# Linear attention and a gated feed-forward net on one core: output by seven half-block products, tails loaded together, a new order

## The chip, the cores and the metric

The kernel runs on one core of one Trainium2 chip. A core has a matrix engine (TensorE, "PE" in the profile, with its weight loads as "PEld"), VectorE ("DVE"), ScalarE ("ACT"), GpSimd ("POOL") and SyncE ("SP"), which here only issues transfers; 16 DMA engines serve the transfer queues. Each engine executes its own instructions in order and waits on semaphores for the others. The metric is the time of one execution in microseconds (us). A lower time is better.

## What is computed

```python
# q, k, v: [8 batches, 8 heads, 576 positions, 64]
phi = lambda x: np.where(x > 0, x, np.exp(x) - 1.0) + 1.0
q_p, k_p = phi(q), phi(k)
kv  = einsum('bhsd,bhse->bhde', k_p, v)      # one 64x64 matrix per batch and head
z   = k_p.sum(axis=2)
x   = einsum('bhsd,bhde->bhse', q_p, kv) / (einsum('bhsd,bhd->bhs', q_p, z)[..., None] + 1e-6)
x   = x.transpose(0, 2, 1, 3).reshape(4608, 512)
a, b = x @ w1, x @ w2                        # 512 -> 1024 each
out  = ((a * b) @ w3) @ w_out                # 1024 -> 1024 -> 512
```

Inputs and the output are float32, 28.3 MB of q, k and v, 10.5 MB of weights and 9.4 MB of output; the products run in bfloat16.

## The kernel before

**Tiling.** A batch has 576 positions: 512 main ones and a tail of 64. The main positions of batch b are chunk b (0 to 7), 512 rows of x; the eight tails make chunk 8. The partition of a main row is position // 4, so that a load has runs of 1 KB.

**Steps.** The program is one long written list of steps, `ORDER`; `manual_schedule` takes each engine's instructions in exactly that order, and the function `step` maps a token to a function. A token is a letter, a batch or chunk number, and an index; one `+` behind it moves a step from its first engine to the next (ScalarE to VectorE for copies, SyncE to GpSimd for loads).

- `M`, `L`, `N` (load_qkv, L92): q, k, v of four heads' main rows, 512 KB each, into the pool `ld` of 13 buffers. `R` (load_tail, L99): tails of one batch. `C`, `E`, `B`: w_out, w3 and column blocks of w1 and w2, all on GpSimd's queue, which converts to bfloat16 on the way.
- `x`/`X`, `y`/`Y`, `z`/`Z` (L164 to L199): phi of k (small letter) or q (capital) as min(exp(x), max(x, 0) + 1): an exponential on ScalarE, a two-operation scalar instruction on VectorE, and a minimum on VectorE. Index 2 is the tail of q and k in one tile.
- `v`: v to bfloat16, with a column of ones beside each head, which gives z in the same matmuls. `K` (kv_full, L216): kv and z of a batch, two heads per matmul. `T`, or `a` through TensorE: phi(q) transposed (T is a DMA transpose on SyncE's queue). `A` (nat, L262): the attention of 128 positions, four matmuls, then 1e-6 added, a reciprocal and a multiplication on VectorE. `D`, or `P` through TensorE: x transposed.
- `w`, `u` (L132, L139): w3 transposed and multiplied with w_out, so that (h @ w3) @ w_out needs only one folded matrix `wf_sb` of 1024x512.
- `F` (f_unit): 128 of the 1024 columns of a and b for a chunk: eight matmuls of 128x512 into two of four PSUM banks, a copy of a on ScalarE (L327) and a multiplication on VectorE (L328). `h` and `i` do the same for F0.0 and F0.1 in quarters.
- `O` (o_unit, L475): 128 rows of the output: eight matmuls of 128x512 over the 1024 columns, and a copy out of PSUM (L481). `S`, `H`: store of two or one row blocks; `Q` (L497): one row block in two halves of 256 columns.

**What sets the order.** SyncE issues its loads, the transposes and the stores strictly in the written order, each behind the wait of the one ahead. GpSimd issues a load once the transfer eight places earlier on its queue has landed. A buffer of a pool is taken round robin and only when its last reader is done. `GATES` names pairs of loads of which the first must wait for the landing of the second; it is empty here.

The file holds functions that the list of this kernel doesn't call: `V` (w_unit, L448), `s` (s_make, L416) and `t` (wt_make, L151) among them. They compute the output of a chunk by Strassen's method in Winograd's form: the 1024 columns of h and the 512 of the output are halved, and so are the 512 rows, and seven products of half blocks replace eight.

Of the kernel before, what the change touches and what calls it, by code (L numbers as in the profile page):

```python
# [8 lines left out]
F32 = mybir.dt.float32  # L9
# [11 lines left out]
def kernel(  # L21
# [24 lines left out]

    consts = ctx.enter_context(tc.tile_pool(name="consts", bufs=1))
    wpool = ctx.enter_context(tc.tile_pool(name="weights", bufs=1))
    ld = ctx.enter_context(tc.tile_pool(name="ld", bufs=13))
    ldr = ctx.enter_context(tc.tile_pool(name="ldr", bufs=3))  # L50
# [4 lines left out]
    xt_p = ctx.enter_context(tc.tile_pool(name="xt", bufs=3))  # L55
# [15 lines left out]
    vrs = [wpool.tile([P, 2, 2, 2, E1], BF16, name=f"vr{i}") for i in range(2)]  # L71
# [5 lines left out]
    def constants(part, alt):  # L77
        if part == 0:
            make_identity(nc, ident)
        else:  # L80
            eng = nc.vector if alt else nc.gpsimd
            for t in (vrs[part - 1], kvs[part - 1]):
                eng.memset(t, 0.0)
            eng.memset(vts[part - 1][..., D:E1], 1.0)
            for g in range(2):
                eng.memset(vrs[part - 1][g * R:(g + 1) * R, :, g, :, D:E1], 1.0)
# [12 lines left out]
    def load_tail(b, part, alt):  # L99
        names = ("qk", "v")[part]  # L100
        t = raw[names + "r", b] = ldr.tile([P, len(names), RW], F32, tag="ldr" + names, name=names + "32r")
        for i, name in enumerate(names):
            for g in range(2):
                ins = (nc.gpsimd if alt else nc.sync).dma_start(  # L104
                    out=t[g * R:(g + 1) * R, i].rearrange("p (h d) -> p h d", d=D),
                    in_=src[name][b, g * 4:(g + 1) * 4, NJ * P:S, :].rearrange("h p d -> p h d"))
# [50 lines left out]
    ph, es = {}, {}  # L157

    def part_of(name, b, g):
        if g == 2:  # L160
            return raw["qkr", b].rearrange("p i x -> p (i x)"), 2 * RW, "r"
        return raw[name, b, g], HW, ""

    def phi_exp(name, b, g):  # L164
        x, w, r = part_of(name, b, g)
        e = e_p.tile([P, w], BF16, tag="e" + r, name="e" + r, bufs=2 if r else 4)
        es[name, b, g] = e
        nc.scalar.activation(out=e, in_=x, func=AF.Exp)  # L168

    def phi_max1(name, b, g, alt):  # L170
        x, w, r = part_of(name, b, g)
        y = es["y", name, b, g] = e_p.tile([P, w], BF16, tag="y" + r, name="y" + r, bufs=2)
        (nc.gpsimd if alt else nc.vector).tensor_scalar(  # L173
            out=y, in0=x, scalar1=0.0, scalar2=1.0, op0=ALU.max, op1=ALU.add)

    def phi_tile(name, b):
        p = ph.setdefault((name, b), [None, None])
        if p[0] is None:
            w = JW + (2 * RW if name == "q" else 0)
            t = phi_p.tile([P, w], BF16, tag=name + "j", name=name + "j", bufs=1 if name == "k" else 2)  # L180
            p[0] = t[:, 0:JW].rearrange("p (c j u d) -> p c j u d", j=NJ, u=2, d=D)
            if name == "q":
                p[1] = t[:, JW:JW + RW]
                ph["qt", b] = t
                ph.setdefault(("k", b), [None, None])[1] = t[:, JW + RW:JW + 2 * RW]
        return p

    def phi_min(name, b, g):
        x, w, r = part_of(name, b, g)
        e, y = es[name, b, g], es["y", name, b, g]  # L190
        if g == 2:
            phi_tile("q", b)
            nc.vector.tensor_tensor(out=ph["qt", b][:, JW:JW + 2 * RW], in0=e, in1=y, op=ALU.min)
            return
        p = phi_tile(name, b)
        e, y = (t.rearrange("p (c u j d) -> p c u j d", c=2, u=2, d=D) for t in (e, y))
        for c in range(2):
            nc.vector.tensor_tensor(out=p[0][:, 2 * g + c].rearrange("p j u d -> p u j d"),  # L198
                                    in0=e[:, c], in1=y[:, c], op=ALU.min)  # L199

    def v_unit(b, i, alt):
        vt, vr = vts[b % 2], vrs[b % 2]
# [4 lines left out]
        else:  # L207
            for g in range(2):
                rows = slice(g * R, (g + 1) * R)
                copy_of(alt)(out=vr[rows, :, g, :, 0:D], in_=raw["vr", b][rows, 0].rearrange(  # L210
                    "p (i u d) -> p i u d", i=2, d=D))
# [4 lines left out]
    def kv_full(b, alt):  # L216
        kj, kr = ph["k", b]
        vt, vr, kv = vts[b % 2], vrs[b % 2], kvs[b % 2]
        kvp = at_ps.tile([P, 2, NCH], F32, tag="at", name="kvp")
        W = 2 * E1  # L220
        for i in range(2):
            for g in range(2):
                hp = 2 * g + i
                for j in range(NJ):
                    nc.tensor.matmul(kvp[:, i, g * W:(g + 1) * W],  # L225
                                     kj[:, hp, j].rearrange("p u d -> p (u d)"),
                                     vt[:, j, 2 * hp:2 * hp + 2, :].rearrange("p h e -> p (h e)"),
                                     start=(g == 0 and j == 0), stop=False, skip_group_check=True)
# [435 lines left out]
```

## Time and profile before

| | |
|---|---|
| time, median of 3 runs (lowest, highest) | 259.99 us (259.03, 260.37) |
| time of the profiled execution | 259.34 us |
| its span, first to last instruction | 257.4 us |
| granted TensorE clock, mean | 0.993 |
| busy: TensorE, VectorE, ScalarE, GpSimd | 232.3, 159.1, 116.8, 49.1 us |
| first matmul, first F, first K | 13.15, 40.70, 26.01 us |
| last matmul ends | about 252.6 us |

The page splits the span into 40 slices of 6.4 us and gives a digit, the busy share in tenths, for each engine. Groups put the instructions of one line and shape together, with total busy time, mean duration of one, and the idle time ahead of them with what ended it. Matmuls overlap in the records: a 128x512 one lasts 380 ns there, but the next starts 216 ns later. A window's row gives, behind its length, the busy time of PE, PEld, DVE, ACT and POOL with the number of instructions, the granted clock, the DMA share and GB/s.

### The profile page before, as it was taken

The page shows a single profiled execution, that of the slowest core. Times are in us where ns is not written, and L with a number is a line of the kernel's source. Part 1 is how long each engine was busy: PE and PEld are TensorE (multiplying, and loading weights), DVE is VectorE, ACT ScalarE, POOL GpSimd, SP SyncE. Part 2 cuts the span into 40 slices and gives each one's busy share as a digit, 9 for nine tenths or more (in the row PEclk, how much of TensorE's full clock was granted, in tenths as well). Part 3 has the DMA queues.
Part 4 walks back from the last instruction along what each step waited for, and adds up shares of the span by engine and source line. Part 5 has one row for each costly group of instructions (what it writes and reads, how often), then busy time and mean ns, then how long its engine had stood idle before and what let it go on. Part 6 is the DMA issues. An engine that isn't in the chain of part 4 may idle for free.

```text
span 257.4 us, 3788 instructions
## 1 busy us (share of the span) xinstructions
PE 232.3 (90%) x1352; PEld 117.8 (46%) x1368; DVE 159.1 (62%) x350; ACT 116.8 (45%) x180; POOL 49.1 (19%) x84
## 2 busy tenths in 40 slices
PE   0087899999999869999999999999999999999992
PEld 0063565554454434445445445454544444444540
DVE  0548589778899426897887899978235633343200
ACT  1404677357756506755562473645332312332221
POOL 8524479455045100600000000000000000000000
PEclk9999999999999979999999999999999999999999
DMA  6999999999989999799999998646512143001124
GB/s 220 211 237 289 311 255 245 200 248 283 299 247 291 194 242 347 182 284 222 356 308 211 289 263 272 154 89 151 200 20 91 74 83 163 3 0 30 42 115 139
DMA packets 63762, 50.57 MB, mean 196 GB/s; under 512 B 33536, under 2 KB 58368, under 8 KB 63744
## 3 DMA queue, kind: packets, MB, share of 16 engines
q1 hardware_dynamic: 54432, 37.10, 55.9%
q0 software_dynamic: 9152, 13.11, 23.4%
q8 instruction: 10, 0.16, 0.3%
q10 hardware_dynamic: 160, 0.13, 0.2%
q14 instruction: 8, 0.07, 0.1%
HBM read 38.80 MB, written 9.44 MB: 187 GB/s over the span
## 4 chain that ended last, share of the span: by engine, by line
PE 78%; DMA 13%; DVE 4%; issue 2%; ACT 0%; POOL 0%; DVEq 0%; ACTq 0%; POOLq 0%
PE a_ps L322 24%; PE b_ps L322 23%; PE o_ps L479 21%; DMA v<-in_v_dram 5%; DMA qt<-qj 4%; PE nd L280 4%; DMA wt_sb<-in_moe_w_out_dram 4%; PE kvp L225 2%; PE wf_ps L143 1%; PE kvp L229 1%; DVE y L173 1%; DVE vt L204 1%; PE o_ps L504 1%; DVE kj L198 1%; DVE qj L198 0%
## 5 line engine op out<-in xcount | busy, mean ns | idle before, releaser
L322 PEld LDWEIGHTS <-w_sb 128*128 128x128 bf16 x576 | 55.3, 98 | 61.8 <-issue 0.9
L328 DVE TENSOR_TENSOR ab<-a_sb,b_ps 128x512 bf16<-128x512 f32 x72 | 49.1, 685 | 38.2 <-PE b_ps L322 30.5
L322 PE MATMUL a_ps<-xt,w_sb 128*128 128x512 bf16 x256 | 67.3, 382 | 0.0
L322 PE MATMUL b_ps<-xt,w_sb 128*128 128x512 bf16 x256 | 66.7, 379 | 0.0
L327 ACT COPY a_sb<-a_ps 128x512 f32<-128x512 f32 x72 | 41.8, 585 | 54.4 <-PE a_ps L322 48.9
L479 PE MATMUL o_ps<-wf_sb,ab 128*128 128x512 bf16 x267 | 63.7, 383 | 0.8 <-issue 0.2
L479 PEld LDWEIGHTS <-ab 128*128 128x128 bf16 x280 | 27.0, 98 | 30.2 <-issue 0.8
L481 ACT COPY o_sb<-o_ps 128x512 f32<-128x512 f32 x29 | 16.8, 585 | 43.4 <-PE o_ps L479 27.2
L286 DVE TENSOR_TENSOR xn<-nd,r 128x512 bf16<-128x512 f32 x32 | 22.1, 691 | 1.1
L168 ACT ACTIVATE e<-q 128x1024 bf16<-128x1024 f32 x16 | 16.7, 1056 | 8.5 <-DMA q<-in_q_dram 8.5
L168 ACT ACTIVATE e<-k 128x1024 bf16<-128x1024 f32 x16 | 16.6, 1056 | 5.2 <-DMA k<-in_k_dram 5.0
L280 PE MATMUL nd<-kv,qt 128*128 128x130 bf16 (+1 forms) x160 | 16.1, 223 | 2.6 <-DMA qt<-qj 2.1
L136 PE MATMUL w3p<-ident,w3b 128*128 128x128 bf16 x64 | 5.7, 242 | 13.7 <-DMA w3b<-in_moe_w_dram 13.7
L280 PEld LDWEIGHTS <-qt 128*128 128x128 bf16 (+1 forms) x160 | 11.6, 101 | 14.0 <-issue 3.3
L284 DVE TENSOR_SCALAR r<-nd 128x8 f32<-128x8 f32 (+1 forms) x40 | 6.5, 162 | 16.8 <-PE nd L280 16.4
L173 DVE TENSOR_SCALAR y<-q 128x1024 bf16<-128x1024 f32 x16 | 11.2, 707 | 8.7 <-DMA q<-in_q_dram 8.7
L143 PE MATMUL wf_ps<-wt_sb,w3t 128*128 128x512 bf16 x61 | 14.9, 380 | 0.7 <-DMA wt_sb<-in_moe_w_out_dram 0.5
L104 POOL DMA_DIRECT2D qk32r<-in_q_dram x14 | 9.0, 648 | 19.1 <-ACT a_sb L327 16.5
L198 DVE TENSOR_TENSOR qj<-e,y 128x512 bf16<-128x512 bf16 x32 | 11.9, 417 | 0.4 <-ACT e L168 0.3
L198 DVE TENSOR_TENSOR kj<-e,y 128x512 bf16<-128x512 bf16 x32 | 11.9, 418 | 0.2
L225 PE MATMUL kvp<-vt,kj 128*128 128x130 bf16 x128 | 9.8, 219 | 2.4 <-DVE vt L204 1.8
L136 PEld LDWEIGHTS <-w3b 128*128 128x128 bf16 x64 | 4.6, 109 | 15.0 <-DMA w3b<-in_moe_w_dram 14.5
(54 smaller groups left out, 180.3 us busy)
## 6 DMA issues: line engine op xcount, KB each, us to landing
out_dram<-o_sb SPq DMA_DIRECT2D x16, 512.0 KB, 3.7
q<-in_q_dram SPq DMA_DIRECT2D x13, 512.0 KB, 8.0
k<-in_k_dram SPq DMA_DIRECT2D x13, 512.0 KB, 6.7
v<-in_v_dram SPq DMA_DIRECT2D x12, 512.0 KB, 8.0
w3b<-in_moe_w_dram POOLq DMA_DIRECT2D x8, 256.0 KB, 12.0
v<-in_v_dram POOLq DMA_DIRECT2D x4, 512.0 KB, 9.8
w_sb<-in_moe_w_dram POOLq DMA_DIRECT2D x8, 256.0 KB, 6.9
q<-in_q_dram POOLq DMA_DIRECT2D x3, 512.0 KB, 11.2
```

The costliest lines, as they stand in the source:

```text
L143: nc.tensor.matmul(wfs[i], w3ts[i][:, kc, :], wo_sb[:, kc, :], start=(kc == 0), stop=(kc == FC - 1))
L168: nc.scalar.activation(out=e, in_=x, func=AF.Exp)
L173: (nc.gpsimd if alt else nc.vector).tensor_scalar(out=y, in0=x, scalar1=0.0, scalar2=1.0, op0=ALU.max, op1=ALU.add)
L198: nc.vector.tensor_tensor(out=p[0][:, 2 * g + c].rearrange("p j u d -> p u j d"), in0=e[:, c], in1=y[:, c], op=ALU.min)
L225: nc.tensor.matmul(kvp[:, i, g * W:(g + 1) * W], kj[:, hp, j].rearrange("p u d -> p (u d)"), vt[:, j, 2 * hp:2 * hp + 2, :].rearrange("p h ...
L280: nc.tensor.matmul(nd[rows, g, i * 2 * E1:(i + 1) * 2 * E1], w, kvs[b % 2][:, i, g].rearrange("p u e -> p (u e)"), start=True, stop=True)
L286: nc.vector.tensor_tensor(out=dst.rearrange("p (g h) e -> p g h e", g=2), in0=v4[:, :, :, 0:D], in1=r[rows].unsqueeze(3).to_broadcast([n, ...
L322: nc.tensor.matmul(ps, w[:, kc, f * P:(f + 1) * P], xt_of(c)[:, :, kc, :], start=(kc == 0), stop=(kc == KC - 1))
L327: nc.scalar.copy(out=a_sb, in_=a_ps)
L328: nc.vector.tensor_mul(out=abs_[c][:, f, :], in0=a_sb, in1=b_ps)
L479: nc.tensor.matmul(o_ps, ab[:, f, m * P:(m + 1) * P], wf_sb[:, f, :], start=(f == 0), stop=(f == FC - 1))
L481: copy_of(alt)(out=rows_of(c, m // 2)[:, m % 2], in_=o_ps)
```

## The change

- **Output of chunks 0 to 7**: the 32 `O` steps of these chunks become seven `V` products each (eight matmuls of 128x256 each), with four `s` steps per chunk (sums and differences of half blocks of h on VectorE) and four `t` steps once (differences of half blocks of the folded weights). Three products of a chunk are copied out by ScalarE, three additions on VectorE join two products, and one product is copied out directly. Chunk 8 keeps `O` and `Q`.
- **Tails**: batches 0 and 1 load their tails each into one half of a tile's partitions; for batches 2 to 7 one set of six loads brings batches 2 to 4 into the lower half and 5 to 7 into the upper half. phi of tails then runs on 64 or 128 partitions of 1024 columns, for two batches at once, and transposes of tails stand alone. The tail's part of `K` becomes four matmuls of 130 columns, with zeros in the half that belongs to the other batch.
- **Zeros**: eight `j` steps of four 128x512 matmuls on a tile of zeros near the beginning of the list.
- **Buffers**: `ld` 13 to 8, `xt` 3 to 2, phi(q) 2 to 1, tail pools changed, small PSUM copies 4 to 5.
- **Order**: a new `ORDER` throughout, and 16 pairs in `GATES`.

```diff
-    ld = ctx.enter_context(tc.tile_pool(name="ld", bufs=13))
-    ldr = ctx.enter_context(tc.tile_pool(name="ldr", bufs=3))
+    ld = ctx.enter_context(tc.tile_pool(name="ld", bufs=8))
+    ldr = ctx.enter_context(tc.tile_pool(name="ldr", bufs=1))
...
-    xt_p = ctx.enter_context(tc.tile_pool(name="xt", bufs=3))
+    xt_p = ctx.enter_context(tc.tile_pool(name="xt", bufs=2))
...
-            for g in range(2):
+            for g in halves:
+                b0 = b + (g * NT if b >= 2 else 0)
                 ins = (nc.gpsimd if alt else nc.sync).dma_start(
-                    out=t[g * R:(g + 1) * R, i].rearrange("p (h d) -> p h d", d=D),
-                    in_=src[name][b, g * 4:(g + 1) * 4, NJ * P:S, :].rearrange("h p d -> p h d"))
+                    out=t[g * R:(g + 1) * R, i].rearrange("p b (h d) -> p (b h) d", d=D),
+                    in_=src[name][b0:b0 + n, :, NJ * P:S, :].rearrange("b h p d -> p (b h) d"))
...
+        for j in range(NJ + 1):
+            for hp in range(KC):
+                g, i = divmod(hp, 2)
+                heads = slice(2 * hp, 2 * hp + 2)
+                if j < NJ:
+                    l, r = kj[:, hp, j].rearrange("p u d -> p (u d)"), vt[:, j, heads, :]
+                else:
+                    l, r = kr[:, hp * P:(hp + 1) * P], vr[:, heads, :]
+                nc.tensor.matmul(kvp[:, i, g * W:(g + 1) * W], l, r.rearrange("p h e -> p (h e)"),
+                                 start=(g == 0 and j == 0), stop=(j == NJ), skip_group_check=True)
...
+    def keep_warm():
+        z = kvs[0].rearrange("p i g u e -> p (i g u e)")
+        t = mm_ps.tile([P, NCH], F32, tag="mm", name="warm")
+        for _ in range(4):
+            nc.tensor.matmul(t, z[:, 0:P], z[:, 0:NCH], start=True, stop=True)
...
     ORDER = """
-    M0.0+ Y0.0 C1 E0 M0.1 I0 X0.0 E3 X0.1 L0.0 Y0.1 Z0.0 Z0.1 C0 y0.0 w0+ R0.0 R0.1 x0.0 E4 x0.2
-    I1 w3+ L0.1+ x0.1 a0.0+ E1 y0.2 a0.1+ N0.1+ u0.2+ N0.0+ z0.0 R1.1 v0.1 y0.1 w4+ u3.2+ E2 w1+
...
-    O8.2 F7.5 H8.2 F7.3 F7.0 Q8.3 O7.0 O7.1 O7.2 S7.0 O7.3 O8.0 S7.1 O8.1 S8.0
+    M0.0+ I1 j0 R0.0+ j1 L0.0+ Y0.0 R0.1+ y0.2 L0.1+ v0.2+ N0.0+ j6 N0.1 j2 v0.1 C0 E5 j5 j7
+    M0.1 X0.0 x0.0 E6 C1 X0.1 E3 I0 Z0.0 Y0.1 x0.2 Z0.1 M1.1+ z0.2 v0.0+ a0.0+ y0.0 E7 x0.1 a0.1
+    y0.1 j4 E0 z0.0 z0.1 j3 L1.1+ K0 w5 A0.3 w6 M1.0+ N1.0+ A0.0 u5.2+ w3+ B0.0 A0.2 u6.2 w7+
+    Y1.1 X1.1 X1.0 u3.2+ I2 B0.1 w0+ L1.0+ A0.1 u7.2 P0.0 y1.1 x1.1 Z1.1 P0.3+ Y1.0 u0.2 z1.1
+    P0.2+ P0.1 R1.0+ v1.0 x1.0 Z1.0 a1.1+ y1.2 y1.0 N1.1+ E4 a1.0 R1.1+ x1.2 h0 z1.0 B3.0 E1 h1
+    L2.1 v1.1 M2.0 M2.1 B3.1 h2 h3 v1.2 L2.0 E2 z1.2 w4+ M3.0 i0 N2.0 i1 K1 u4.2 A1.0 w1+ F0.6
+    w2 B2.1 A1.3 B1.0 F0.7 P1.0+ B1.1 A1.1 x2.1 P1.3+ u1.2 A1.2 u2.2 y2.1 z2.1 t0 Y2.0 F0.3 B2.0
+    X2.0 t1 t2 F0.2 P1.2 R2.0+ Z2.0 s0.0 P1.1 T0.1 F0.5 Y2.1 t3 X2.1 Z2.1 F0.4 M3.1 F1.2 s0.1
+    y2.0 R2.1+ N2.1 s0.2 x2.0 z2.0 T2.0 L3.1 s0.3 V0.1 F1.6 F1.1 L3.0 y3.2 V0.2 x3.2 z3.2 y2.2
...
+    D3.1 V6.4 V6.5 F7.4 V6.6 D4.1 V6.7 F7.7 F7.2 S6.0 F8.6 V7.1 s7.1 s7.2 F8.0 V7.4 S6.1 s7.0
+    s7.3 V7.3 F8.7 V7.6 V7.5 V7.2 S7.0 F8.3 F8.1 F8.2 V7.7 F8.4 S7.1 F8.5 O8.0+ O8.1 S8.0 Q8.3
+    O8.2 H8.2
     """
-    GATES = ""
+    GATES = "E0<C1 E1<B0.0 B1.0<M1.0 L1.1<L0.0 B1.1<N1.0 B2.0<L1.0 B2.1<N1.0 B3.0<L1.1 B3.1<E0 L2.0<L1.1 N2.0<M2.0 L2.1<E1 M2.0<L1.0 M2.1<L0.0 L3.1<L1.1 N3.1<C1"
```

## Prediction

> **What bounds the kernel now.** I read the shares of the engines and the slices first, then the chain that ended last, the groups, and at last time windows cut where batch 2's and batch 7's KV products end.
>
> ```profile
> PE 232.3 (90%) x1352; PEld 117.8 (46%) x1368; DVE 159.1 (62%) x350; ACT 116.8 (45%) x180; POOL 49.1 (19%) x84
> ...
> PE   0087899999999869999999999999999999999992
> ...
> DVE  0548589778899426897887899978235633343200
> ...
> DMA  6999999999989999799999998646512143001124
> ...
> HBM read 38.80 MB, written 9.44 MB: 187 GB/s over the span
> ...
> PE 78%; DMA 13%; DVE 4%; issue 2%; ACT 0%; POOL 0%; DVEq 0%; ACTq 0%; POOLq 0%
> ...
> L328 DVE TENSOR_TENSOR ab<-a_sb,b_ps 128x512 bf16<-128x512 f32 x72 | 49.1, 685 | 38.2 <-PE b_ps L322 30.5
> ...
> L479 PE MATMUL o_ps<-wf_sb,ab 128*128 128x512 bf16 x267 | 63.7, 383 | 0.8 <-issue 0.2
> ...
> L198 DVE TENSOR_TENSOR kj<-e,y 128x512 bf16<-128x512 bf16 x32 | 11.9, 418 | 0.2
> ```
> TensorE has nothing to do for 13 us and is then hardly ever idle; VectorE and the DMA engines are also nearly full until about 180 us. So the end is TensorE's start, plus its work, plus its few stalls.
>
> ```profile
> 0.00:27.50 27.50, 11.70 (x91) 7.62 (x93) 12.62 (x25) 7.45 (x8) 14.97 (x30) 1.00 1.02 245
> 27.50:46.50 19.00, 18.09 (x154) 11.16 (x155) 15.65 (x35) 14.11 (x21) 13.64 (x22) 1.00 1.20 259
> 46.50:74.70 28.20, 28.15 (x171) 14.03 (x170) 23.48 (x55) 15.71 (x24) 9.49 (x16) 1.00 1.16 249
> 74.70:182.10 107.40, 104.08 (x602) 51.96 (x607) 84.03 (x194) 56.83 (x87) 10.95 (x18) 0.98 0.96 242
> 182.10:252.70 70.60, 70.26 (x344) 32.99 (x347) 23.35 (x42) 22.13 (x40) 0.00 (x0) 1.00 0.23 77
> ```
> Columns: length; busy time of TensorE, its weight loads, VectorE, ScalarE, GpSimd; clock; DMA share; GB/s. I call 0 to 74.7 the head (up to K2), 74.7 to 182.1 the middle (K2 to K7), 182.1 to 252.7 the rest; 4.7 us of copy and store follow. Two more looks, at TensorE's order of time and GpSimd's:
>
> ```profile
> 15.43 2.00 PE L257 MATMUL tp<-ident,qj 128*128 128x128 bf16 x16
> ...
> 40.26 0.61 PE L257 MATMUL tp<-ident,qj 128*128 128x128 bf16 x8
> ...
> 92.23 0.40 PE L280 MATMUL nd<-kv,qt 128*128 128x130 bf16 x4 [2.10 <-DMA qt<-qj]
> 92.47 2.86 PE L479 MATMUL o_ps<-wf_sb,ab 128*128 128x512 bf16 x8
> ...
> 240.35 1.91 PE L504 MATMUL o_ps<-wf_sb,ab 128*128 128x256 bf16 x16
> 242.10 10.52 PE L479 MATMUL o_ps<-wf_sb,ab 128*128 128x512 bf16 x47
> ```
> ```profile
> 26.60 0.63 POOL L104 DMA_DIRECT2D qk32r<-in_q_dram  x1 [0.34 <-DMA w3b<-in_moe_w_dram]
> ...
> 37.64 1.01 POOL L95 DMA_DIRECT2D v<-in_v_dram  x1 [1.15 <-DMA k<-in_k_dram]
> ```
> From starts to starts: a 128x256 matmul takes 0.109 us (16 from 240.35 to 242.10), a 128x512 one 0.2155 (0.86 us for each four in the chain). An F unit (8 matmuls) is then 1.725, an old output unit O 1.725, a product V 8 x 0.109 = 0.873, K about 1.15, A 0.23, a w3 transpose unit 0.445. On VectorE, likewise: 0.62 for a 128x512 operation on PSUM or a 128x1024 bf16/one-input one, 1.04 for the three of an A, 0.70 for a pair of minimums.
>
> **The change, part by part.**
>
> *Products.* Removed: 32 O units (256 matmuls, 32 x 1.725 = 55.2 us). Added: 56 products, 448 matmuls of 128x256, 56 x 0.873 = 48.9. TensorE gains 6.3 us. The price asks for a weight load each 0.109 us: each matmul has one, and these loads take 98 ns in the groups, so there is 11 ns to spare. The Trainium skill speaks against this part: "TensorE: Matmul & The Clock Gate", Back-to-back issue gap, gives a sustained 81 ns for a matmul of 128 columns and 131 for one of 512, since weight loads set the pace with them. Read between those, a 256-wide one is an estimate of 98 ns, and the products would lose 448 x 0.098 - 256 x 0.131 = 10.4 us. This trace doesn't agree: 215.5 and 109 ns, exactly half, so I keep 6.3.
>
> VectorE pays: per chunk four half-block sums or differences (128x1024 bf16, two inputs) and three additions from PSUM, once four differences of the weights. No row has a two-input bf16 operation of 1024: lower bound 0.62 (the one-input 128x1024 rows), upper 0.75 (two 128x512 minimums); I take 0.62, since one instruction has one start-up. That is 8 x 7 x 0.62 + 4 x 0.62 = 37.2 us, less 6 old output copies. ScalarE makes 32 copies for chunks 0 to 7 instead of 26, 6 x 0.585 = 3.5 us in all, on an engine 45% busy: nothing.
>
> *Tails.* 48 loads of 64 KB become 6 of 128 KB and 6 of 384 KB, the same bytes. 40 of them were GpSimd's, at 0.62 to 0.65 us of issue; that engine is empty after 100 us, so the issue saves nothing on the path. VectorE's tail work stays even (16 at about 0.41 become 10 at about 0.63), V copies fall from 16 to 8. A wait is added: the exponentials for batches 2 and 3 wait for all four q/k tail loads (1.57 MB), which GpSimd issues last; queued behind them on ScalarE are the copies of F1.5 and later. On KV, 32 matmuls of 130 columns replace 16 of 260: even.
>
> *Zeros.* 32 matmuls, 6.9 us at full clock. 24 stand ahead of the first transposes and 8 ahead of K0; both need batch 0, so TensorE is idle there in either case: nothing, unless batch 0 lands before 10 us (it can't, below). The row at 15.43 (16 transposes in 2.00 us, later 8 in 0.61) and the slow group after the stall at 92.23 (2.86 us for 1.73) show that TensorE is slow for some us after it idled. The Trainium skill (same page, Part 1) says the clock is halved until some 3.4 us of activity; by that rule the zeros are worth about 2 us, and the result below would be 253. In my sum they are worth nothing, as what follows them waits for loads.
>
> *Order, head.* Here I expect a loss. GpSimd waits at the 9th transfer for the 1st, and so on, so its waits give landings: at 26.6 us 11 of its transfers and SP's first loads were in (6.8 + 1.4 MB), at 37.6 18 of them (10.5 + 1.4 MB): 0.35 MB/us from 3 us on. The new queue brings batch 0 first (3.54 MB: 13.3 us; K0, after 4 us of VectorE work, ends at about 19, before at 27.5), but then w_out and w3 (5.1 MB for the first transposes, 17.6 us; 6.7 MB for the first folding, 22 us) with batch 1 between them, and w1/w2 late: their first columns make 11.4 MB (35.6 us), and the blocks that F0.6, F0.2 and F0.4 need come after E1, from where SP's held loads of batch 2 (L2.1<E1 holds its whole queue) run beside them. F0.6 wants 15 MB (45 to 46 us; it started at 40.7 before), F0.3 and F0.2 17.1 MB, plus up to 2.6 MB of batch 2 that came between: 52 to 59 us. Work to the end of K2 is the same in both orders, 54.3 us (61.2 less 6.9 of zeros). So K2 ends later: bounds 74.7 (the old time, if loads are no tighter) and 83 (the two queues share the DMA evenly from 43 us: last block of w1 and w2 at 62 to 64 us, 18 us of F, V and K behind it). I take 79.5, just above the middle, as the rate of 0.35 is measured and only the sharing is not.
>
> *Order, middle.* TensorE: 30 F, 31 products, 5 K, 24 A: 51.8 + 27.1 + 5.8 + 5.5 = 90.1 us (before 34 F, 18 O: 101.2, measured 107.4). VectorE: its 84.0 us, plus 16 sums and 13 additions (18.0), less 4 F, one A, 4 copies, and savings on tails and v copies (11 to 12): 90 us. Two in-order engines with 90 us each. The best stretches of before ran VectorE at 18.3 and 18.7 of 20 us with TensorE full, so 90 us of it need 96 at that rate; but its last 3 us aren't needed by K7, hence 93. Bounds: 90.1, and 101 (89% of VectorE). Before's stall of 4 to 5 us at 84 to 97 (vt, then the transposed q after a long DMA) goes with the old order; what is late next is VectorE. Buffers for q, k, v fall from 13 to 8, so 5 x 0.524 MB or 7.5 us of loading less can lie ahead; a batch of six fits, and the DMA share falls from 1.0 to 0.4 only after 160 us, so I cost this at nothing: its cover is the 20 us between a batch's load and its K, and what it costs without cover lies inside the 101.
>
> *Rest.* 27 F, 23 products, 6 A, three O, the split last one: 75.0 by count, against 70.2 before, because more F is left behind K7. VectorE has 37 us there. Before ran 0.4 above its count: 75.3. The last copy and store: 4.7 as before, with one row block.
>
> Sum: 79.5 + 93 + 75.3 + 4.7 = 252.5 of span, against 257.4. Outside the span 259.34 - 257.4 = 1.9: **254.4 us**, against 259.34 of that run, whose time lies 0.25% under the median 259.99. By the median it is 255.0, which I give.
>
> **Rivals.**
> 1. Head as before and VectorE keeping up: 74.7 + 90.5 + 75.3 + 4.7 + 1.9 + 0.6 = 247.7. For it: both orders move the same bytes, and TensorE is warm. Against: the w1/w2 blocks stand further back.
> 2. Slower: VectorE becomes the bound of the middle. Place: F's multiplication and V's additions queue behind sums and minimums, so PSUM banks come free late (four for F, shared with two of the products). Price: 103 us in place of 93 (VectorE 87% busy): 265. From 98 on, together with my head, the gain is gone. For it: slices of 9 with less work; against: 0.93 reached twice.
> 3. Loads late: K2 at 86, by batch 2's loads shared evenly with w1/w2 and the q/k tails at the end of GpSimd's queue: 261.5. For it: DMA share 1.0 to 1.2 all through the head.
> 4. Narrow matmuls are paced by their weight loads and not by their columns, so that products cost more than O units. If just 30 of the 98 ns of a load showed, 448 x 0.03 = 13.4 us: 268. Against it stands the row at 240.35, with the same shapes and no gap; it decides from 14 ns on. (The skill's figures above would give 255.0 + 6.3 + 10.4 = 272.)
>
> **Chances.** Forecast 46%, rival 1 17%, rival 2 18%, rival 3 16%, rival 4 3%. Range 246.5 to 264.5 leaves out some 2 in 10; the likeliest case alone spans 251 to 259. About 0.5% (258.7 to 261.3) is what this kernel's measurement tells from no change. Faster: nearly all of 46 and 17, 0.60; within: 0.13 (edges of the forecast and rival 3); slower: 0.27.
>
> **What would show it.** Right: K0 near 18 to 20 us, first F at about 45, K2 ending at 78 to 81, the K2-K7 stretch 91 to 96 with VectorE above 90% busy, about 75 after it, products at 0.109 a matmul. Wrong: a PE idle of several us for DMA w_sb or qk32r after 45 us (rival 3), waits of PE on ab or on PSUM evacuations by DVE in the middle (rival 2), or no stalls at all (rival 1).

## The result and the profile after

The changed kernel takes 268.52 us (median of 4 runs, 267.14 to 268.84); the kernel before, on the same chip, 259.83. The ratio is 1.033 (95% interval 1.028 to 1.037): 8.7 us slower, outside the range of the prediction. Medians here and below are of all executions of a kernel, while ratios and their intervals leave out executions more than 1.5% above its fastest. The profiled execution took 268.84 us, its span is 267.1 us, the mean clock 0.978.

From the page of the changed kernel, its shares, slices, chain and groups:

```profile
PE 238.8 (89%) x1603; PEld 140.2 (53%) x1608; DVE 184.1 (69%) x382; ACT 129.2 (48%) x191; POOL 35.7 (13%) x58
...
PE   4768988996199999989996998999999999999992
...
PEclk9997999999869999999999999999999999999998
...
PE 53%; DMA 30%; DVE 5%; POOL 4%; ACT 3%; issue 3%; SPq 0%; DVEq 0%; ACTq 0%; POOLq 0%
...
L337 PE MATMUL a_ps<-xt,w_sb 128*128 128x512 bf16 x256 | 68.1, 385 | 7.0 <-ACT a_sb L342 5.5
...
L190 ACT ACTIVATE e<-q 128x1024 bf16<-128x1024 f32 x16 | 16.9, 1056 | 24.2 <-DMA q<-in_q_dram 24.1
...
L456 PE MATMUL u<-wt_sb,s 128*128 128x256 bf16 x128 | 16.6, 273 | 0.0
...
L444 DVE TENSOR_TENSOR s<-ab 128x1024 bf16<-128x1024 bf16 x16 | 10.8, 685 | 0.0
```

TensorE has work from the first slices on (the zeros), but there is a hole in the eleventh slice, at about 67 to 73 us, with a low clock behind it. In the chain TensorE's share went from 78% to 53% and that of transfers from 13% to 30%. ScalarE waited 24 us for q ahead of the exponentials, against 8.5 in the kernel before:

```profile
L168 ACT ACTIVATE e<-q 128x1024 bf16<-128x1024 f32 x16 | 16.7, 1056 | 8.5 <-DMA q<-in_q_dram 8.5
```
The new lines themselves, products (L456) and sums (L444), show no idle time ahead of them.

Windows of the changed kernel, cut at the ends of K2 (89.3) and K7 (187.0); columns as before (length; busy time of TensorE, its weight loads, VectorE, ScalarE, GpSimd; clock; DMA share; GB/s):

```profile
0.00:44.00 44.00, 33.87 (x238) 19.25 (x241) 24.59 (x53) 23.00 (x28) 29.94 (x52) 0.96 1.07 249
44.00:61.00 17.00, 15.80 (x106) 8.49 (x108) 10.10 (x24) 6.64 (x12) 5.74 (x6) 1.00 1.22 216
61.00:72.00 11.00, 5.57 (x28) 2.72 (x28) 5.14 (x10) 3.17 (x6) 0.00 (x0) 0.95 1.08 201
72.00:89.30 17.30, 15.68 (x86) 7.72 (x86) 16.45 (x33) 12.57 (x18) 0.00 (x0) 0.84 1.11 288
89.30:187.00 97.70, 92.55 (x686) 58.01 (x685) 87.25 (x196) 58.87 (x87) 0.00 (x0) 1.00 0.98 226
187.00:262.40 75.40, 75.33 (x463) 44.05 (x462) 40.61 (x71) 24.36 (x42) 0.00 (x0) 1.00 0.26 83
```

| stage | before | forecast | after |
|---|---|---|---|
| head, to K2's end | 74.7 | 79.5 | 89.3 |
| middle, K2 to K7 | 107.4 | 93 | 97.7 |
| rest | 70.6 | 75.3 | 75.4 |
| last copy and store | 4.7 | 4.7 | 4.7 |
| span | 257.4 | 252.5 | 267.1 |

Against the kernel before the head loses 14.6 us, the middle gains 9.7, the rest loses 4.8, +9.7 in all. Against the forecast the head misses by 9.8 us and the middle by 4.7.

What stands in the hole is seen in the order of time of the changed kernel, engine by engine (start, length, line, what ended the idle time before it): TensorE, ScalarE, VectorE, SyncE, GpSimd.

```profile
62.19 1.02 PE L337 MATMUL b_ps<-xt,w_sb 128*128 128x512 bf16 x4 [2.27 <-DVE ab L343]
...
73.30 1.87 PE L337 MATMUL a_ps<-xt,w_sb 128*128 128x512 bf16 x4 [5.54 <-ACT a_sb L342]
74.96 1.91 PE L337 MATMUL b_ps<-xt,w_sb 128*128 128x512 bf16 x4
...
78.01 1.03 PE L337 MATMUL b_ps<-xt,w_sb 128*128 128x512 bf16 x4
...
71.72 1.06 ACT L190 ACTIVATE e<-q 128x1024 bf16<-128x1024 f32 x1 [7.83 <-DMA q<-in_q_dram]
72.69 1.05 ACT L342 COPY a_sb<-a_ps 128x512 f32<-128x512 f32 x2
...
71.66 0.69 DVE L195 TENSOR_SCALAR y<-q 128x1024 bf16<-128x1024 f32 x1 [5.86 <-DMA q<-in_q_dram]
...
45.37 1.38 SPq L106 DMA_DIRECT2D q<-in_q_dram  x2
...
44.50 1.95 POOL L123 DMA_DIRECT2D qk32r<-in_q_dram  x2 [0.78 <-issue]
...
51.87 0.95 POOL L123 DMA_DIRECT2D v32r<-in_v_dram  x1 [1.96 <-DMA w_sb<-in_moe_w_dram]
```

Read it backwards. TensorE stops since its PSUM banks are full; the copy that would free one (L342) is queued on ScalarE behind an exponential of batch 2's q, which waits 7.83 us for its load. SyncE had issued both q loads of batch 2 by 46.8; the second lands at 71.7, 25 us later. Between 44.5 and 52.8 GpSimd had issued the six big tail loads, 2.36 MB for batches 2 to 7. Then TensorE starts at the low clock (1.87 to 1.91 us for four matmuls that take 1.03 otherwise): the twelve from 73.30 to 78.01 us took 4.71 us, 2.1 more than at 0.2155 each. The two waits of TensorE (5.54 and 2.27 us) and this slow start come to 9.9 us, about as much as the head misses its forecast by. From issue to landing the tail loads took:

```profile
qk32r<-in_q_dram POOLq DMA_DIRECT2D x2, 384.0 KB, 17.6
qk32r<-in_k_dram POOLq DMA_DIRECT2D x2, 384.0 KB, 20.6
v32r<-in_v_dram POOLq DMA_DIRECT2D x2, 384.0 KB, 22.7
```

Summed from the packets of the traces (weights count as written, in bfloat16): between 50 and 70 us of the span SyncE's queue moved 1.5 MB (1.3 to 2.7) and GpSimd's 2.7 MB (10.9 to 13.6); before it was 4.2 (1.6 to 5.8) and 1.2.

### The profile page after: what moved, and what is told of

The parts are those of the page before. It is cut to its first block, busy times and chain, and to the rows that moved or that the text cites. A ratio compares the mean times of both kernels' runs of the same rounds, so it can differ in the third digit from the quotient of the medians.

```text
span 267.1 us, 4296 instructions
## 1 busy us (share of the span) xinstructions
PE 238.8 (89%) x1603; PEld 140.2 (53%) x1608; DVE 184.1 (69%) x382; ACT 129.2 (48%) x191; POOL 35.7 (13%) x58
## 4 chain that ended last, share of the span: by engine, by line
PE 53%; DMA 30%; DVE 5%; POOL 4%; ACT 3%; issue 3%; SPq 0%; DVEq 0%; ACTq 0%; POOLq 0%
PE a_ps L337 15%; PE b_ps L337 15%; DMA q<-in_q_dram 14%; PE u L456 9%; PE t L456 6%; DMA wt_sb<-in_moe_w_out_dram 4%; DMA v32r<-in_v_dram 4%; DMA v<-in_v_dram 3%; DMA out_dram<-o_sb 3%; DMA xt<-xn 3%; PE nd L295 2%; PE kvp L245 2%; PE o_ps L500 2%; ACT e L190 1%; DVE y L195 1%
## 5 line engine op out<-in xcount | busy, mean ns | idle before, releaser
L337 PE MATMUL b_ps<-xt,w_sb 128*128 128x512 bf16 x256 | 67.6, 383 | 4.0 <-DVE ab L343 2.3
L342 ACT COPY a_sb<-a_ps 128x512 f32<-128x512 f32 x72 | 41.8, 584 | 55.1 <-PE a_ps L337 51.8
L456 PEld LDWEIGHTS <-s 128*128 128x128 bf16 x256 | 24.5, 98 | 6.2 <-DVE s L444 0.8
L195 DVE TENSOR_SCALAR y<-q 128x1024 bf16<-128x1024 f32 x16 | 11.1, 696 | 18.3 <-DMA q<-in_q_dram 18.2
L456 PEld LDWEIGHTS <-ab 128*128 128x128 bf16 x192 | 18.5, 98 | 4.5
L218 ACT CAST vt<-v 128x1024 bf16<-128x1024 f32 x15 | 15.8, 1051 | 3.7 <-DMA v<-in_v_dram 3.6
L456 PE MATMUL u<-wt_sb,s 128*128 128x256 bf16 x128 | 16.6, 273 | 0.0
L162 PE MATMUL wf_ps<-wt_sb,w3t 128*128 128x512 bf16 x60 | 14.6, 379 | 0.4 <-ACT a_sb L342 0.2
L295 PE MATMUL nd<-kv,qt 128*128 128x130 bf16 x128 | 12.7, 222 | 2.0 <-DVE xn L301 2.0
L431 PE MATMUL warm<-kv 128*128 128x512 bf16 x32 | 10.0, 484 | 3.7 <-POOL kv L94 3.7
L295 PEld LDWEIGHTS <-qt 128*128 128x128 bf16 x128 | 9.2, 98 | 7.1 <-DVE xn L301 4.6
L195 DVE TENSOR_SCALAR y<-k 128x1024 bf16<-128x1024 f32 x16 | 10.9, 690 | 0.0
L444 DVE TENSOR_TENSOR s<-ab 128x1024 bf16<-128x1024 bf16 x16 | 10.8, 685 | 0.0
```

Source lines behind the costliest of these rows:

```text
L162: nc.tensor.matmul(wfs[i], w3ts[i][:, kc, :], wo_sb[:, kc, :], start=(kc == 0), stop=(kc == FC - 1))
L195: (nc.gpsimd if alt else nc.vector).tensor_scalar(out=like(y, rows, g), in0=x, scalar1=0.0, scalar2=1.0, op0=ALU.max, op1=ALU.add)
L218: copy_of(alt)(out=vt[:, :, 4 * i:4 * i + 4, 0:D], in_=raw["v", b, i].rearrange("p (h j d) -> p j h d", h=H // 2, j=NJ))
L295: nc.tensor.matmul(nd[rows, g, i * 2 * E1:(i + 1) * 2 * E1], w, kvs[b % 2][:, i, g].rearrange("p u e -> p (u e)"), start=True, stop=True)
L337: nc.tensor.matmul(ps, w[:, kc, f * P:(f + 1) * P], xt_of(c)[:, :, kc, :], start=(kc == 0), stop=(kc == KC - 1))
L342: nc.scalar.copy(out=a_sb, in_=a_ps)
```

## The experiments

Two theories for the head. A: the tails of six batches, loaded at once in front of batch 2, take the transfer time that batch 2's q needed. B: the gate L2.1<E1 holds SyncE's queue for too long, so batch 2 is asked for too late. Beside that: what products, zeros and order are worth alone. Each kernel is the changed one with one edit, unless it says otherwise; the runs are called e1, e2 and so on; medians and intervals are against runs of the kernel before on the same chip.

### Tails in three sets (e1)

```diff
-   ... R2.0+ ... R2.1+        (six loads of 384 KB, batches 2 to 7)
+   ... R2.0+ ... R2.1+ ... R3.0+ R3.1+ ... R4.0+ R4.1+   (18 loads of 128 KB, two batches a set)
+   GATES: R3.0<N2.1 R4.0<N3.1;  y3.2 x3.2 z3.2 moved behind z3.1
```

> The changed kernel, but the tails of batches 2 to 7 come in three sets (2 and 5, 3 and 6, 4 and 7), the second held until the last v load of batch 2 has landed, the third until that of batch 3. Same tiles, same bytes. Theory A (1.6 MB of tails that nobody needs yet crowd out the q loads of batch 2 between 55 and 72 us): the q load that landed at 71.7 us lands at about 63, K2 ends near 80 instead of 89.3, time about 260. Rival B (batch 2's loads are simply started too late, by the gate on L2.1): K2 within 2 us of 89, time 266 to 269. Rival C (VectorE is the bound, loads don't matter): K2 earlier, but the time gained is lost again before K7, 266 to 269.

Measured: 265.9 us, ratio 1.019 (1.012 to 1.025); span 262.2. Its windows, cut at K2 and K7, and its two longest waits in the middle:

```profile
0.00:80.80 80.80, 67.54 (x457) 36.73 (x462) 54.93 (x115) 44.31 (x60) 39.24 (x64) 0.98 1.12 249
80.80:182.00 101.20, 92.83 (x688) 58.13 (x686) 88.68 (x197) 60.03 (x88) 4.07 (x6) 1.00 1.01 236
182.00:257.50 75.50, 75.45 (x466) 44.14 (x463) 40.65 (x71) 24.42 (x42) 0.00 (x0) 1.00 0.25 81
```
```profile
88.51 1.03 PE L458 MATMUL t<-wf_sb,s 128*128 128x256 bf16 x8 [2.33 <-ACT p L464]
...
98.02 1.03 PE L458 MATMUL u<-wt_sb,s 128*128 128x256 bf16 x8 [2.97 <-ACT p L464]
```

K2 ends at 80.8 instead of 89.3: A holds for the head, which is nearly what I had forecast. SyncE's queue moved 3.8 MB between 50 and 70 us (1.5 in the changed kernel), GpSimd's 1.0 (2.7). A's time of 260 was missed: the middle is 3.5 us longer, so that 4.9 of the 8.5 us reach the end of the span, and 2.6 us the median (the profiled execution, 263.98 us, was the fastest). The loads are also smaller here, 128 KB each and not 384; this wasn't separated from when they come.

### The gate taken away (e2)

```diff
-    GATES = "... N2.0<M2.0 L2.1<E1 M2.0<L1.0 ..."
+    GATES = "... N2.0<M2.0 M2.0<L1.0 ..."
```

> The changed kernel without the pair L2.1<E1, so that SyncE's queue isn't held until 44.8 us; the other pairs stay. Rival B: batch 2's loads start by 36 us at the latest, both q loads have landed by 60, no wait of TensorE between 58 and 73 us, K2 ends near 78, time about 258. Theory A: they start earlier, but w1, w2 and w3 blocks are delayed by as much and the tails still stand in the way of what follows: K2 at 85 to 89, time 264 to 269.

Measured: 268.06 us, ratio 1.031 (1.026 to 1.036), K2 at 89.8. TensorE's waits of that kernel (total, times, longest):

```profile
PE b_ps L337 <- DMA w_sb<-in_moe_w_dram: 3.3, 2, 1.8
PE a_ps L337 <- DMA w_sb<-in_moe_w_dram: 2.9, 1, 2.9
```

At 50 us SyncE's queue had moved 2.5 MB (1.3 in the changed kernel) and GpSimd's 10.2 (10.9): batch 2 comes earlier, and w3 and w1/w2 later. The gate isn't the cause; B falls.

### Old output blocks in the new order (e4)

```diff
-   V.2, V.6, V.5, V.7 of each chunk;  V.1 V.3 V.4, all s and t
+   O.0, O.1,  O.2, O.3
```

> The changed kernel with the output of chunks 0 to 7 by four O units per chunk again: at the places of V.2, V.6, V.5 and V.7 the units O.0 to O.3, the other products, the s and the t steps left out. If products are worth on TensorE what they save in matmul time (6.3 us) and cost nothing on VectorE: the stretch behind K7 is 2 to 3 us longer, and the time 272 to 275. If VectorE's 37 us of sums and additions make the middle late: the time falls, to 262 to 267. If stalls hide either: 267 to 270.

Measured: 281.55 us, ratio 1.082 (1.078 to 1.086). Its rows of middle and rest:

```profile
91.00:192.50 101.50, 95.12 (x567) 47.57 (x574) 70.60 (x166) 58.59 (x86) 0.00 (x0) 1.00 0.86 214
192.50:274.40 81.90, 79.69 (x387) 36.99 (x391) 26.75 (x49) 24.99 (x43) 0.00 (x0) 1.00 0.22 70
```
That is above all three of my ranges. In the new order the products are worth 13 us, twice their saving in matmul time: 6.5 us of them in the rest (81.9 against 75.4), where 14 blocks stand in place of 23 products and TensorE is idle for 2.2 us, the others ahead of it. Not all of this is the products' own: by the profiles TensorE is busy 7.5 us longer here and idle 4.5 us longer, and 4.0 us of its waits are for copies of the `O` units themselves, which stand in an order written for products. The other parts of the change together cost 21 us against the kernel before, with the `O` units so placed.

### The products in the kernel before (e6)

```diff
-    ld bufs=13;  O0.3 ... O0.2 ... O0.1 ... O0.0        (each chunk 0 to 7)
+    ld bufs=12;  s0.0 s0.1 s0.2 s0.3 V0.1 V0.2 ... V0.3 V0.4 ... V0.5 V0.6 ... V0.7
```

> The kernel before with the products alone: every group of four O units of chunks 0 to 7 becomes seven products in the same places, sums ahead of the first, the t steps once, stores of a chunk not ahead of its last product, and 12 buffers for q, k, v instead of 13 to make room. If the products save 6.3 us of TensorE and VectorE keeps up: about 254. If VectorE can't keep up in the middle (84 + 20 us in 107): 258 to 264.

Measured: 278.17 us, ratio 1.068 (1.063 to 1.073). Its windows up to K7, and TensorE's waits:

```profile
0.00:80.20 80.20, 58.89 (x428) 34.40 (x432) 57.40 (x124) 38.17 (x54) 38.20 (x67) 1.00 1.04 233
80.20:198.70 118.50, 103.20 (x712) 62.61 (x710) 101.18 (x223) 59.30 (x90) 10.76 (x18) 0.97 0.89 220
```
```profile
PE u L435 <- DVE s L423: 7.9, 4, 3.4
PE u L435 <- ACT p L441: 3.9, 1, 3.9
```

Here the products cost 18 us, far above both of my ranges: VectorE has 101 us to do in the middle instead of 84, TensorE waits for its sums, the middle grows by 11.1 and the head by 5.5. One buffer less and the stores moved behind the last products are part of this edit, and one placing of the products was tried. With these orders the products alone are a loss, the other parts without them are a loss, and together they lose least. The new order leaves 4.8 us more of TensorE's work behind K7, where VectorE has room, and its middle asks 87 us of VectorE and not 101.

### No zeros (e3)

```diff
-   M0.0+ I1 j0 R0.0+ j1 L0.0+ ... j6 N0.1 j2 v0.1 C0 E5 j5 j7 ... j4 ... j3
+   M0.0+ I1 R0.0+ L0.0+ ... N0.1 v0.1 C0 E5 ...
```

> The changed kernel without the eight steps of matmuls on zeros. If, as I costed them, they only fill time in which TensorE waits for batch 0, the time stays within 1 us of the changed kernel's 268.5. If the slow clock after idling costs what it seemed to (16 transposes in 2.0 us and not 1.2), K0 and the first folding matmuls come out 1 to 2 us later, and the time is 269.5 to 270.5.

Measured: 269.92 us, ratio 1.031 (1.021 to 1.042). The median lies in the range of a slow clock, but the executions (266.5 to 270.7) cover both ranges and those of the changed kernel. Rows of this run:

```profile
13.71 2.14 PE L271 MATMUL tp<-ident,qj 128*128 128x128 bf16 x16 [13.71 <-POOL ident masks.py:199]
18.48 2.59 PE L245 MATMUL kvp<-vt,kj 128*128 128x130 bf16 x16 [2.63 <-DVE kj L211]
```

The first 16 transposes take 2.14 us in one row; with zeros they take 0.61 and 0.73, so the zeros do make them faster. But K0 begins at 18.48 us in both, and its first 16 matmuls take 2.59 us without zeros and 2.52 with them (1.10 later on): by then TensorE is slow either way. In the single profiles K2 ends at 92.8 without zeros and 89.3 with them, and the span differs by 0.9 us; a worth of 0 to 2 us for the zeros can't be told apart.

### Tails in pairs, later sets let go earlier (e7)

```diff
-   GATES: R3.0<N2.1 R4.0<N3.1
+   GATES: R3.0<M2.1 R4.0<N2.1
```

> The tails in three sets as in the run before with that name, but the second set is released by the landing of q load M2.1 and the third by that of v load N2.1, one batch earlier each. Theory: K2 stays near 81 us as there, and the two waits of 2 to 3 us at 86 to 98 us (ScalarE held by exponentials of tails that have just been issued, copies of products behind them) go: the stretch K2 to K7 falls from 101 to 96 or 97, time 261. Rival (the middle is VectorE's in any case, and what is gained ahead of K2 is lost there): 264 to 266.

Measured: 266.15 us, ratio 1.017 (1.007 to 1.027); the profiled execution, its fastest, took 263.05. K2 ends at 78.4 and K7 at 181.1: a middle of 102.7. The order of time of TensorE, ScalarE and SyncE shows its longest wait and where it comes from:

```profile
93.26 1.86 PE L458 MATMUL u<-wf_sb,ab 128*128 128x256 bf16 x8 [4.90 <-ACT o_sb L496]
...
90.73 1.05 ACT L220 CAST vt<-v 128x1024 bf16<-128x1024 f32 x1 [5.53 <-DMA v<-in_v_dram]
...
64.38 11.27 SPq L265 DMA_TRANSPOSE qt<-qj  x1
75.75 1.09 SPq L106 DMA_DIRECT2D k<-in_k_dram  x2
```

My number for the middle missed. The same pattern as in the head comes again one batch later: ScalarE stands at a load (v of batch 3), and behind it a copy that TensorE needs. That load was issued at 77.5 because SyncE stood 11.27 us at one transposing transfer (T2.0), though what it reads was ready.

### Batch 2's q later in the engines' order (e8)

```diff
-   Y2.0 X2.0 Z2.0 Y2.1 X2.1 Z2.1 ... T2.0 ... F1.6 F1.1
+   ... F1.6 F1.1 Y2.0 X2.0 Z2.0 Y2.1 X2.1 Z2.1 T2.0        (tails as in the changed kernel)
```

> The changed kernel with the six phi steps of batch 2's q and its DMA transpose moved behind F1.1, so that no copy of F0.5 to F1.1 stands behind a wait for the late q loads on ScalarE or VectorE; loads unchanged. Theory D (it is the place of the waits in the two in-order engines that stops TensorE, not the lateness itself): no wait of TensorE between 58 and 73 us, K2 at 80 to 82, time 259 to 262. Rival (the tails' exponentials and the transposed q, also late, take their place): K2 at 86 to 89, time 265 to 268.

Measured: 268.22 us, ratio 1.029 (1.021 to 1.037), K2 at 89.9. TensorE's stop moved:

```profile
75.86 1.87 PE L456 MATMUL t<-wf_sb,ab 128*128 128x256 bf16 x8 [7.15 <-ACT a_sb L342]
...
73.79 1.06 ACT L190 ACTIVATE e<-k 128x1024 bf16<-128x1024 f32 x1 [9.65 <-DMA k<-in_k_dram]
```

The rival was right, with K2 and the time just above its bounds: another late load, batch 2's k, takes the place of q. So moving the steps in the engines' lists doesn't help while the loads stay late.

### Two sums of each chunk on GpSimd (e10)

```diff
-   s1.0 s1.1 ... s4.0 s4.1
+   s1.0+ s1.1+ ... s4.0+ s4.1+
```

> The changed kernel with the first two of the four sums of chunks 1 to 4 on GpSimd, which has nothing to do after 52 us: 8 of the 16 sums in the middle, 5 us of VectorE's 87. If VectorE is what the middle (97.7 us) ends on, it shrinks by 2 to 4 us, time 265 to 266. If the chain of the sums is slower there and products wait for it, or if loads bind the middle: 268 to 272.

Measured: 271.48 us, in two pairs (269.1 and 269.5, 273.4 and 273.9), so I give no ratio. The middle was 99.7 us (87.9 to 187.6), no shorter than 97.7, and TensorE waited 4.0 us for sums; whether loads would have held it anyway, this run can't say. GpSimd was idle there, but a sum takes it over three times as long as the 0.68 us of VectorE (shortest, median and longest in ns, from the view of the tile):

```profile
L444 POOL TENSOR_TENSOR s<-ab x8: 2125/2234/3111, 92.1 to 165.6; 128x1024 bf16<-128x1024 bf16 x8
```

### The transposing transfer behind the loads, then through TensorE (e11, e14, e15, e16)

From the kernel with early pairs (e7). First T2.0 behind batch 3's loads; then batch 2's query transposed by TensorE; then batch 3's as well; then one output unit of the end moved forward.

```diff
-   z2.0 T2.0 L3.1 s0.3 V0.1 F1.6 F1.1 L3.0 ... N3.0 ... N3.1      (e7)
+   z2.0 L3.1 s0.3 V0.1 F1.6 F1.1 L3.0 ... N3.0 ... N3.1 T2.0      (e11)
+   z2.0 L3.1 s0.3 F1.6 a2.0 a2.1 V0.1 F1.1 L3.0 ...               (e14)
+   e14, and:  s1.1 T3.0 x3.1 v3.0 V0.5 A2.0  ->  s1.1 a3.0 x3.1 v3.0 V0.5 A2.0 a3.1   (e15)
+   e15, and:  O8.0+ O8.1 S8.0 Q8.3  ->  O8.0+ Q8.3 O8.1 S8.0       (e16)
```

> The kernel with tails in pairs and early gates (e7), with one step moved: the whole-query transpose of batch 2 (T2.0) goes behind the loads of batch 3 in SyncE's order, so that its wait for the feature map (SyncE stood 11.27 us at it) no longer holds those loads. Theory B (the hold on SyncE's queue is the next wait): batch 3's loads are issued near 64 us instead of 75 to 79, the wait of 4.90 us in the output products and the 5.53 us wait for v on ScalarE go, K2 stays near 78, the middle falls from 102.7 to about 97, and the time from 266.2 to about 261. Rival (the transfers themselves are the limit: in every variant so far K7 ended at 181 to 187 us and the same bytes had landed by any given time): the wait moves to the next load, K7 still ends at 180 or later, time 264.5 to 267.

Measured: 273.86 us, ratio 1.057 (1.052 to 1.061). The loads did go out earlier, but the transfer again held SyncE for 11.75 us, now later, and both TensorE and VectorE (whose next q tile has one buffer) stood until it was done:

```profile
92.79 0.61 PE L297 MATMUL nd<-kv,qt 128*128 128x130 bf16 x4 [13.16 <-DMA qt<-qj]
...
92.77 0.42 DVE L213 TENSOR_TENSOR qj<-e,y 128x512 bf16<-128x512 bf16 x1 [15.15 <-DMA qt<-qj]
...
76.49 11.75 SPq L265 DMA_TRANSPOSE qt<-qj  x1
```

My theory fell as I had put it, and the time lies above the rival's range too: this isn't a wait for the feature map, which in e7 was ready by 64.3 us. The packets show what it goes with: the transfer's own, 2048 of 256 bytes, start at 86.5 us, 1.75 us before SyncE is free again, and until then SyncE's queue moves the 1-KB packets of the loads ahead of it. In e7 it is the same: they start at 73.7 us, and SyncE is free at 75.65.

> The kernel with tails in pairs and early gates (e7), with batch 2's query transposed by TensorE (16 transposes, two copies on ScalarE, as for batches 0 and 1) instead of by SyncE's transfer. The run before showed that this transfer occupies SyncE's queue until the loads issued ahead of it have moved (11.27 us in e7, 11.75 us where more loads stood ahead of it), and that its position only chooses what is late. Theory (queue order behind that transfer is the rest of the loss): batch 3's loads go out near 64 us, nothing waits for the transfer, the wait of 4.90 us goes, TensorE pays some 1.5 us for the transposes: the middle falls from 102.7 to about 98 to 99, time about 262. Rival (the rate of the transfers is the limit whatever stands in front): another load is late by as much, the middle stays at 101 to 104, time 265 to 268.

Measured: 262.56 us, ratio 1.007 (1.003 to 1.010), 3.6 us under e7 by the medians, though the intervals overlap. The time is the theory's; the middle, 101.3 in the profiled execution (263.95 us, slower than the median), is the rival's. There one wait of several us was left, behind the next such transfer:

```profile
81.69 10.66 SPq L265 DMA_TRANSPOSE qt<-qj  x1
...
93.08 3.34 SPq L328 DMA_TRANSPOSE xt<-xn  x1
...
100.36 1.10 PE L339 MATMUL a_ps<-xt,w_sb 128*128 128x512 bf16 x4 [4.51 <-DMA xt<-xn]
```

> As the kernel before it (e14), with batch 3's query transposed by TensorE as well. There SyncE stood 10.66 us at that transfer (81.69 to 92.35 us), the transposition of batch 2's normalized rows behind it went out at 93.1, and TensorE waited 4.51 us for it at 100.4, followed by some 2 us of matmuls at the low clock; it was its only wait of over 1.6 us between K2 and K7. Theory (the transposing transfers in SyncE's queue are what holds the middle up): that wait goes, TensorE pays about 1.5 us for the transposes, the middle falls from 101.3 to 96 to 98, the time from 262.6 to about 258.5, under the kernel before. Rival (the rate of the transfers is the limit): the next load becomes the wait of 3 to 5 us and the middle stays at 100 to 103, time 261 to 264.

Measured: 263.96 us, ratio 1.016 (1.011 to 1.021). In the profiled execution (261.6, its fastest) the middle is 97.1, as the theory said, and no wait above 1.3 us is left in it; but the median rose by 1.4 us, and the interval of the ratio lies above that of e14. At the end of that profile ScalarE's last copy stands behind two late store issues:

```profile
251.52 3.40 ACTq L536 DMA_DIRECT2D out_dram<-o_sb  x2
254.96 0.58 ACT L504 COPY o_sb<-o_ps 128x512 f32<-128x512 f32 x1 [3.47 <-issue]
```

> As the kernel before it (e15), with one output unit of the end moved forward, so that the two stores that ScalarE issues no longer stand in front of its last copy. In the profile of e15 these two issues took 3.40 us (1.20 in the changed kernel and in e14), the last copy waited 3.47 us for them, and the last store was issued at 255.6 instead of near 253.3. Theory (that late issue is what hid e15's shorter middle): the end is 2 us shorter, the median falls from 264.0 to about 261.5 and lies at or under e14's 262.6. Rival (the issue was late in the profiled execution alone, and e15's other executions lost their time elsewhere): the median stays at 263 to 265.5.

Measured: 262.39 us, ratio 1.011 (1.007 to 1.015). The issues took 1.25 us here, and the median fell by 1.6, nearly as the theory said, with intervals that overlap. Windows of the profiled execution (260.46 us):

```profile
0.00:80.60 80.60, 68.03 (x474) 37.86 (x479) 54.97 (x115) 46.36 (x62) 41.59 (x68) 0.98 1.11 249
80.60:176.80 96.20, 93.14 (x702) 59.45 (x700) 88.78 (x197) 61.65 (x90) 1.91 (x3) 1.00 0.98 240
```

In these single profiles the middle falls from 101.3 to 97.1 and 96.2 once batch 3's query, like batch 2's, is no longer transposed through SyncE's queue. That this is worth anything in time isn't shown: e14's profile is of an execution above its median, those of e15 and e16 of their fastest, e15 is slower than e14 by the ratios, and a version's executions lie 3 to 7 us apart. The step from e7 (266.15) to the three versions at 262.4 to 264.0 is seen in the medians alone. All of them remain above the kernel before, by 0.7 to 1.6%.

### Products only where VectorE is free (e12, e13)

In the kernel before, only chunks 5 and 6 (then 5, 6 and 7) by products, behind K7; the sums lie in load buffers that are free by then, and some units of chunk 8 are moved in between the products. Of the edit, chunk 5:

```diff
-    O5.0 F6.3 S4.0 O5.1 A7.4 ... O5.2 O5.3
+    t0 t1 t2 t3 s5.1 s5.2 s5.0 s5.3 V5.1 V5.2 F6.3 S4.0 V5.3 V5.4 A7.4 ... V5.5 V5.6 V5.7
```

> The kernel before with only chunks 5 and 6 computed by seven products, where VectorE has room (behind K7 it is busy a third of the time); the four sums use load buffers that are free by then, so no buffer is taken away. Theory A (the products gain what their matmul time says wherever VectorE has room): 4 x 1.725 = 6.90 us of output blocks become 7 x 0.873 = 6.11 us in each chunk, 1.6 us less in all: about 258.4 us, ratio 0.994. Rival (the chain of sums and copies, 0.7 us each, stalls TensorE in the products by as much as they save): 259.5 to 262, with waits for s or p1 shown at the product line.

Measured: 259.24 us, ratio 1.000 (0.997 to 1.004). TensorE's waits at the products come to 0.5 us in the rest, and yet the 1.6 us of matmul time don't show in the time; my 0.994 lies outside the interval. Where they went, I haven't found.

> As before, but chunks 5, 6 and 7 by seven products; chunk 7 is the end of the kernel, with little other work of TensorE beside it, and a store of 512 KB comes last. Theory A: 3 x 0.79 = 2.4 us less, about 257.6 us. Rival: the seven products of the last chunk stand in one row and wait for their copies (each product 0.87 us, copy and semaphore about 0.9), some 1 to 3 us of waits and a later last store: 258.5 to 261, and above the version with chunks 5 and 6 alone.

Measured: 260.6 us, ratio 1.006 (1.003 to 1.008): 0.6% above the kernel before, as the rival said. TensorE's four waits for output copies in the rest come to 2.4 us, what the products should have saved. No version tried beats the kernel before.

## Why the prediction was wrong

**The step that failed is the head**, "I take 79.5", with its bound of 83 from "the two queues share the DMA evenly". It measured 89.3. I had counted when the blocks of w1 and w2 would land, and this went right: K0 began at 18.5 us (forecast 18 to 20; it ended at 21.5 and not at 19), F0.6 at 46.4 (45 to 46). What I missed stood in the part on the tails: I called the loads "the same bytes" and priced their issue and VectorE's work, but not the time that they take from other transfers. The 2.36 MB of tails were the same bytes at another time, in front of what the next F units and exponentials needed, and the sharing was far from even: 1.5 MB for SyncE's queue against 2.7 for GpSimd's between 50 and 70 us. In the packets of the changed kernel between 56 and 68 us the queues do stand even by number, 507 of SyncE's and 506 of GpSimd's. But SyncE's were nearly all of 1 KB, 0.50 MB in all and 56 us of the DMA engines' time, while 419 of GpSimd's were of 4 KB, 1.72 MB and 147 us in all. The Trainium skill ("DMA: Bandwidth & Descriptors", Queues, rings and completion order) says that a DMA engine takes turns between the queues packet by packet. These counts agree, and I hadn't used the rule. With the tails in pairs K2 ends at 80.8 and 78.4, on both sides of my 79.5. I had named what stands behind the tails on ScalarE, and looked for the wait at the tails' own exponentials; it came at batch 2's main q.

**The middle** measured 97.7 for 93, inside its bounds of 90.1 and 101. VectorE's work was 87 us (forecast 90). I had derived 96 from the better of two stretches of before (18.65 of 20 us gives 96.5; the other, 18.29, gives 98.4) and then taken 3 us off for work that K7 doesn't need. TensorE was busy for 92.6 us there where I had counted 90.1, so 93 left it no wait at all; its waits came to 5.1 us. In e2, e3 and e8, which have the same steps in this stretch, the middle was 96.0, 95.1 and 94.8 in the profiled executions. So the number was short by 2 to 5 us, and which part of it failed isn't settled.

**Right**: the rest (75.4 for 75.3), the last copy and store (4.7), the new sums on VectorE (685 ns in the groups, as long as the 128x1024 rows that I took), and the products' own pace: eight matmuls of 128x256 each 0.87 us. The sustained figures of the Trainium skill ("TensorE: Matmul & The Clock Gate", Back-to-back issue gap), from which the products would have lost 10.4 us, don't fit these runs; with weight loads of 98 ns under every matmul the products gain, 13 us in this order by e4.

**Zeros** at nothing: not contradicted by e3, and not shown either, as its executions lie too far apart. K0 began at the same time without them, which is what I had argued. The rule of the same page of the Trainium skill, Part 1, that the clock rises only after some us of activity, agrees with the faster first transposes; the 2 us that would follow from it for the time can't be seen in these runs.

**The 6.3 us** of the products were sized by TensorE alone. What they are worth hangs on VectorE and on the order around them: a gain of 13 us in the new order, a loss of 18 in the old one, nothing behind K7.

**Rivals.** Rival 3 named the place and half of the cause (batch 2's loads beside w1/w2, "the q/k tails at the end of GpSimd's queue") and was too small: K2 at 86, and the middle left at 93. Its chance of 16% was too low: I had leaned on the rate of 0.35 MB per us, measured where nearly all loads were GpSimd's. Rival 1 fell with the head, and rival 4 with the products' pace. Of the kernels with the new order and products, only e7 and e11 had a middle of 102.7 us or more, with a transposing transfer behind the longest wait and not VectorE. Fewer load buffers, costed at nothing, were not tried alone.

## What to carry to other kernels

When loads are joined or moved, ask for each of them what is then in flight in front of it, on every queue, and which in-order engine stands at the late one; equal bytes at another time cost 8.5 us at K2 here. An algorithm that trades matmuls for vector work is worth what the other engine's free time allows: the same seven products gained 13 us, made no difference and lost 18 us in three places, with one order tried in each. And a wait taken away in a stretch where the transfers are full shows up at the next load: three of the repairs here gained at K2 and had given back a third or more by K7.

## What the runs showed of the hardware that I had not expected

- A transposing transfer of a whole query occupies its issuing queue for 1.7 to 2.1 us where no load is in flight (1.89 us at 94.9 in e11, 1.69 at 171.9 in e14) and for 10.7 to 12.3 us behind several loads of 512 KB on the same queue (e7, e11, e14). Nearly all of its own packets move only from 1.6 to 2.2 us before the queue is free again, behind those of the loads; no run varied this alone. The changed kernel had it too: 8.65 us at 63.3 for a transposition of tails and 6.35 at 74.4.
- GpSimd's loads of tails, made of pieces of 256 bytes, took 17.6 to 22.7 us from issue to landing at 384 KB and 8 to 11 us at 128 KB (medians, in e1, e7 and e14). While they moved, GpSimd's 4-KB packets took 334 ns in the median (56 to 68 us) and SyncE's 1-KB packets beside them 111 ns; between 20 and 28 us, when weights and whole batches moved, GpSimd's took 159 ns, and between 84 and 88 us SyncE's alone took 46 ns. In the changed kernel the DMA share was 1.08 between 61 and 72 us at 201 GB/s, and 1.11 at 288 GB/s in the window after: a full share says little about the rate.
- On GpSimd a two-input bf16 sum of 128x1024 took 2.2 us, on VectorE 0.68.
- ScalarE's issue of two stores took 3.40 us in the profile of e15 and 1.20 to 1.25 us in those of e14 and e16. Why is open.
